# Attention and two MoE layers in one program: unread products in the first tiles, an earlier key copy, and a bound on the narrowing

## The chip, the core and the metric

The kernel runs on one core of a Trainium2 chip. The core has a matmul engine (TensorE, PE in the rows), a vector engine (VectorE, DVE), a scalar engine (ScalarE, ACT), a general engine (GpSimd, POOL) and a queue engine that starts transfers (SyncE, SP). Each runs its own instructions in order; semaphores tie them together. The metric is the device time of one execution in microseconds (us), as the median of several.

## What is computed

Four batches, eight heads, 576 positions, head size 64. Attention with rotated queries and keys feeds two dense layers, all in float32:

```python
q_rot, k_rot = rotate(q), rotate(k)
scores = scale * np.matmul(q_rot, k_rot.transpose(0, 1, 3, 2))
scores = scores - np.max(scores, axis=-1, keepdims=True)
attn = np.exp(scores)
attn = attn / (np.sum(attn, axis=-1, keepdims=True) + 1e-09)
x = np.matmul(attn, v)                      # then to (2304, 512)
h = np.maximum(np.maximum(x @ w1, x @ w2), x @ w3)   # 512 -> 768
x = h @ w_out                                        # 768 -> 512
h = x @ w_in                                         # 512 -> 2048
out = (h * (1.0 / (1.0 + np.exp(-h)))) @ w_out2      # 2048 -> 512
```

## The kernel before

**Attention.** Heads are worked on in pairs; a pair is a batch and two heads. `load_qk` brings queries and keys of a pair, `qk_rope` rotates them (on VectorE for pair 0 and half of pair 1, on GpSimd for the rest), and `qk_turn` transposes them on TensorE into a tile `T` and two small tiles with blocks on the diagonal, `K` (`kd`) and `Q` (`qd`), which serve the last 64 positions of both heads. The tail of a pair (positions 512 to 575) is one more transposition into a PSUM tile `tr`, from which ScalarE copies a part of `T` and the two blocks of `Q`, and VectorE the two blocks of `K`. The two engines' copies out of one PSUM tile follow each other in the order of the program text.

A tile is 128 queries of a pair. The first tiles, numbered here from 0, are tiles 0 and 1 of pair 0, then two of pair 1, two of pair 2 and two of pair 3; behind those come the three remaining ones of each pair. Tile 10 is a small one. `attention` runs one step per tile: `tile_scores` (matmuls L387 and L390 into `s`, of which there is one buffer of three PSUM banks), `tile_max` (VectorE's reduction L400 and two exponentials L407 on ScalarE), `tile_norm` of the tile before (reciprocal L417 and two scalings L419) and `tile_turn` of the one before that: nine transpositions L448 in three groups through `tr`, which has two buffers, each group copied to `pt` by ScalarE (L452) or VectorE (L454). After every two tiles of a pair, `av` multiplies by V (L463, L467).

**The weights.** They come as 64-bit floats. W1, W2 and W3 together are twelve pieces, called pieces 0 to 11 here. `narrowing` takes them to 32 bits in a pipeline, one stage further at each step: `narrow_a` (L214 on ScalarE, and then L216 on GpSimd, or L218 on ScalarE for piece 0), `narrow_b` (L225 and L226 on VectorE), `measure` (L140 on ScalarE, a bound on the size). There are four landing buffers, so the transfer of piece n + 4 waits for L226 of piece n. Six pieces give a scale, by `all_max`, and are then split in a high and a low half of 16 bits (L160 on GpSimd, L163 on VectorE); only then real products of the first layer can run. `prep_w1` does one such step for each tile, two from the ninth on.

**What sets the order.** The program text is recorded, and a scheduler then lays out each engine's order with a model of the time. `tc.issue_after(x)` bars an instruction from being placed before `x` in that order. `last` is a dictionary of such marks: `last["max"]` is the newest row maximum, `last["T"]` the newest copy of `T` by ScalarE. PSUM tiles with the tag `m` (two buffers of the ring `ps_m`) serve `all_max` and the first layer.

Of the kernel before, what the change touches and what calls it, by code (L numbers as in the profile page):

```python
# [7 lines left out]
F32 = mybir.dt.float32  # L8
F16 = mybir.dt.float16
I32 = mybir.dt.int32  # L10
U16 = mybir.dt.uint16
AF = mybir.ActivationFunctionType
# [5 lines left out]
P = 128  # L18
# [4 lines left out]
def fused_kernel(  # L23
# [22 lines left out]
    nc = tc.nc  # L46
# [105 lines left out]
    def flat(t):  # L152
        return t.rearrange("p a b -> p (a b)")
# [183 lines left out]
    def qk_turn(b, hp):  # L337


        t = raw_t.pop((b, hp))  # L340
        T = t_p.tile([P, 576 + 512], F32, tag="T", name="T")
        K, Q = kd[(NP * b + hp) % NK], qd[(NP * b + hp) % NK]
        for i in (1, 0):
            tr = ps_t.tile([P, 512], F32, tag="tr", name="tr")
            for c in range(4):
                behind = tc.issue_after(last["s"]) if b == 0 and hp > 1 else nullcontext()
                with behind:
                    nc.tensor.transpose(tr[:, c * P:(c + 1) * P], flat(t[:, 8 * i + 2 * c:8 * i + 2 * c + 2, :]), ident)
            if i == 0:
                last["T"] = nc.scalar.activation(out=T[:, 0:512], in_=tr, func=AF.Copy, scale=0.125).ins  # L350
            else:
                nc.vector.tensor_copy(out=T[:, 512:1024], in_=tr)
        tr = ps_t.tile([P, 512], F32, tag="tr", name="tr")
        nc.tensor.transpose(tr[:, 0:P], flat(t[:, 16:18, :]), ident)
        nc.scalar.activation(out=T[:, 1024:1088], in_=tr[:, 64:128], func=AF.Copy)
        rs = (slice(0, 64), slice(64, 128))
        for r in rs:
            nc.scalar.activation(out=Q[r, r], in_=tr[r, 0:64], func=AF.Copy, scale=0.125)
        for r in rs:
            last["kd"] = nc.vector.tensor_copy(out=K[r, r], in_=tr[r, 64:128]).ins  # L360
        T_t[b, hp] = T, K, Q


# [11 lines left out]
    def tile_scores(key):  # L375
# [2 lines left out]
        s = ps_s.tile([P, 1536], F32, tag="s", name="s")  # L378
        if t == 4:
            nc.tensor.matmul(s[:, 0:512], Q, T[:, 512:1024], start=True, stop=True)  # L380
            nc.tensor.matmul(s[:, 512:576], Q, T[:, 1024:1088], start=True, stop=True)
            s_t[key] = s
            return
        n = P
# [3 lines left out]
        for g, o in ((0, 0), (1, 1024)):  # L388
            r = slice(64 * g, 64 * g + 64)
            last["s"] = nc.tensor.matmul(s[:, o:o + 512], qs[r], kt[r], start=True, stop=True).ins  # L390
        s_t[key] = s

    def heads(key):
# [27 lines left out]
    def tile_turn(key):  # L421
# [9 lines left out]
        if t == 4:  # L431
# [5 lines left out]
            nc.vector.tensor_copy(out=pt[:, 5:9, o:o + 64], in_=t4[:, :, 1])  # L437
            tr = ps_t.tile([P, 512], F32, tag="tr", name="tr")
            nc.tensor.transpose(tr[:, 0:P], e[:, 448:576], ident)
            nc.tensor.transpose(tr[0:64, P:2 * P], e[:, 512:576], ident)  # L440
            nc.scalar.activation(out=pt[0:64, 4, o:o + 64], in_=tr[0:64, P:P + 64], func=AF.Copy)
            nc.vector.tensor_copy(out=pt[64:128, 4, o:o + 64], in_=tr[64:128, 64:128])
            return
        for j in range(3):
            tr = ps_t.tile([P, 512], F32, tag="tr", name="tr")
            for i in range(3):
                c = 3 * j + i
                nc.tensor.transpose(tr[:, i * n:(i + 1) * n], e[0:n, c * P:(c + 1) * P], ident[0:n, 0:n])  # L448
            to, of = pt[:, 3 * j:3 * j + 3, o:o + n], tr[:, 0:3 * n].rearrange("p (a n) -> p a n", a=3)
            evacs[0] += 1  # L450
            if evacs[0] % 3 == 1 if evacs[0] < 28 else evacs[0] % 3:
# [47 lines left out]
    for b in range(1, B):  # L499
# [3 lines left out]
            at(u - 2, v_max, b, hp)  # L503
        at(u, v_scale, b)

    def attention():

        for j in range(len(tiles) + 4):
# [6 lines left out]
                tile_turn(tiles[j - 2])  # L515
            for f, a in events.pop(j, ()):
                f(*a)
            yield


# [101 lines left out]
    def narrowing(W, stage, srcs, queue, lo=0, hi=None):  # L622
# [3 lines left out]
        for n in range(lo, hi + 3):  # L626
            if n < hi:
                r[n] = queue(n, W, stage(n), srcs[n])
            if lo < n <= hi:
                W.narrow_a(n - 1, r[n - 1], pool=n > lo + 1 or lo > 0)  # L630
            if lo + 2 <= n <= hi + 1:
                with tc.issue_after(last["max"]):
                    W.narrow_b(n - 2, r[n - 2])
# [503 lines left out]
    for hp in range(NP):  # L1137
        load_v(0, hp)
    last["max"] = qk_rope(*pairs[0]).ins
    qk_turn(*pairs[0])  # L1140
    wprep = prep_w1(stage1)
    for j in sorted(e for e in events if e < 0):
        for f, a in events.pop(j):
# [133 lines left out]
```

## Time and profile before

| | us |
|---|---|
| median of 3 runs | 1037.62 |
| lowest, highest | 1037.03, 1039.41 |
| the profiled execution | 1035.59 |
| its span in the profile | 1033.9 |

| engine | busy us | share of the span |
|---|---|---|
| TensorE | 962.4 | 93% |
| VectorE | 688.3 | 67% |
| ScalarE | 616.3 | 60% |
| GpSimd | 489.6 | 47% |

The span is what the profile covers from the first instruction to the last; 1.7 us of the execution lie around it. Times in the rows count from the span's start. Shares are averages over the whole span, while the change touches its first tenth, so the section of rows below has stretches and timelines of that tenth. In a timeline, what stands in brackets is how long the engine was idle before the row and what ended that. TensorE's clock has two levels; the column PEclk gives the granted one as a share of the upper. In the first 20 us the column reads 1.00, since no change of the clock is recorded before; the durations there are those of the lower level (2.08 us for four matmuls L390 that take 1.13 at the upper).

### The profile page before, as it was taken

To read this page: it belongs to the slowest core of one execution; us is meant where nothing else is said; L and a number is where in the kernel's file an instruction comes from. 1 tells how busy PE (TensorE), PEld (TensorE's weight loads), DVE (VectorE), ACT (ScalarE), POOL (GpSimd) and SP (SyncE) were. 2 spreads that over 40 slices of the span, in tenths; PEclk is the share of its full clock that TensorE was granted. 3 is DMA by queue.
4 is the path that set the end of the run, shared out by engine and by line. 5 is a ranking of instruction groups with operands and counts; after the bars stand their busy time and mean duration, and the time that the engine had idled before them with its cause. 6 is when DMAs were issued, how large, how long until landed. Compare 5 with 4: busy or idle time off the path is not lost.

```text
span 1033.9 us, 19511 instructions
## 1 busy us (share of the span) xinstructions
PE 962.4 (93%) x7234; PEld 717.0 (69%) x7234; DVE 688.3 (67%) x1295; ACT 616.3 (60%) x1377; POOL 489.6 (47%) x548
## 2 busy tenths in 40 slices
PE   4677998999999999998999999999999999999997
PEld 2343664666666766655756668777888888888887
DVE  6769877765567655687566646645678767867454
ACT  3778676566666575867767754534455644644352
POOL 6735593961127720354223205536258457346164
PEclk9688999999999999999999999999999999999999
DMA  6943132422334510653444415254345244342201
GB/s 152 280 115 101 33 97 75 129 71 62 102 109 110 137 47 27 189 147 118 144 123 139 143 58 168 82 187 145 128 144 168 92 152 125 108 129 93 90 3 41
DMA packets 126062, 117.99 MB, mean 114 GB/s; under 512 B 47376, under 2 KB 109584, under 8 KB 125968
## 3 DMA queue, kind: packets, MB, share of 16 engines
q1 hardware_dynamic: 124464, 116.03, 37.4%
q8 instruction: 57, 0.93, 0.4%
q10 hardware_dynamic: 1504, 0.72, 0.3%
q14 instruction: 37, 0.30, 0.1%
HBM read 90.51 MB, written 26.21 MB: 113 GB/s over the span
## 4 chain that ended last, share of the span: by engine, by line
PE 62%; DVE 9%; ACT 6%; POOL 6%; DMA 6%; issue 3%; SPq 1%; ACTq 0%; DVEq 0%; POOLq 0%
PE m L538 18%; PE xp L467 6%; PE m L946 5%; PE s L390 5%; PE tr L448 5%; PE mb L946 4%; POOL gsum L893 4%; PE mg L538 3%; PE c L1010 3%; PE a L1010 2%; PE b L1010 2%; POOL yr L981 2%; DVE nb L400 1%; PE d L1010 1%; DVE g L898 1%
## 5 line engine op out<-in xcount | busy, mean ns | idle before, releaser
L538 PEld LDWEIGHTS <-w 128*128 128x128 f16 x1632 | 157.3, 98 | 68.8 <-issue 27.8
L538 PE MATMUL m<-x,w 128*128 128x256 f16 (+1 forms) x1336 | 189.7, 288 | 9.9 <-ACT t L554 4.0
L1010 PEld LDWEIGHTS <-g 128*128 128x128 f16 x1485 | 145.7, 98 | 19.9 <-issue 2.3
L946 PEld LDWEIGHTS <-w8s 128*128 128x128 f16 x1344 | 131.4, 98 | 20.3 <-issue 4.8
L400 DVE TENSOR_REDUCE nb<-s 128x2 f32<-128x1152 f32 (+1 forms) x80 | 98.7, 1234 | 49.4 <-PE s L390 39.5
L212 POOL TENSOR_SCALAR z<-z 128x256 uint16<-128x256 uint16 x64 | 56.0, 875 | 159.2 <-DVE z L211 148.4
L407 ACT ACTIVATE e<-s,nb 128x576 f32<-128x576 f32 x144 | 105.1, 735 | 29.0 <-DVE nb L400 24.9
L419 ACT ACTIVATE e<-e,rec 128x576 f32<-128x576 f32 x144 | 104.5, 768 | 17.8 <-DVE rec L417 17.5
L448 PE MATMUL tr<-ident,e 128*128 128x128 f32 x576 | 97.4, 289 | 14.2 <-ACT T L350 6.2
L787 POOL TENSOR_TENSOR z<-z 128x128 f32<-128x128 f32 (+1 forms) x96 | 59.0, 634 | 105.5 <-DMA z<-zwo 38.4
L448 PEld LDWEIGHTS tr<-ident,e 128*128 128x128 f32 x576 | 69.8, 147 | 50.0 <-issue 13.4
L946 PE MATMUL m<-yr,w8s 128*128 128x256 f16 x768 | 90.8, 273 | 3.7 <-DVE t L952 3.7
L452 ACT ACTIVATE pt<-tr 128x384 f32<-128x384 f32 x119 | 56.8, 486 | 47.9 <-PE tr L448 47.7
L467 PE MATMUL xp<-pt,vd 128*64 128x256 f32 (+1 forms) x512 | 84.6, 419 | 0.0
L390 PE MATMUL s<-T 64*128 64x512 f32 x256 | 83.7, 698 | 0.0
L960 POOL TENSOR_TENSOR z<-t 128x256 f32<-128x256 f32 x32 | 28.0, 875 | 95.8 <-DVE t L952 55.9
L946 PE MATMUL mb<-yr,w8s 128*128 128x256 f16 x576 | 69.9, 274 | 2.3 <-ACT yr L158 2.1
L538 PE MATMUL m<-h,wo 128*128 128x256 f16 (+1 forms) x448 | 64.9, 286 | 0.1
L898 DVE SCALAR_TENSOR_TENSOR g<-gsum,sg,g 128x1024 f16<-128x1024 f32 x36 | 49.1, 1373 | 22.1 <-ACT g L897 21.6
L538 PEld LDWEIGHTS <-wo 128*128 128x128 f16 x512 | 49.3, 98 | 16.9 <-issue 4.0
L897 ACT ACTIVATE g<-gsum,sg 128x1024 f16<-128x1024 f32 x36 | 40.7, 1140 | 32.8 <-POOL gsum L893 32.8
L330 POOL TENSOR_TENSOR w<-qk,sin_sb 128x384 f32<-128x384 f32 (+1 forms) x44 | 45.7, 1058 | 30.4 <-DMA qk<-in_q_dram 16.0
(231 smaller groups left out, 1910.8 us busy)
## 6 DMA issues: line engine op xcount, KB each, us to landing
w8s<-w8scr SPq DMA_DIRECT2D x64, 448.0 KB, 4.2
z<-in_moe_w_in_dram SPq DMA_DIRECT2D x32, 256.0 KB, 3.2
z<-in_moe_w_out_dram SPq DMA_DIRECT2D x32, 256.0 KB, 3.3
w<-in_moe_w_dram SPq DMA_DIRECT2D x6, 768.0 KB, 6.0
wo<-in_moe_w_dram SPq DMA_DIRECT2D x6, 768.0 KB, 4.6
qk<-in_q_dram SPq DMA_DIRECT2D x32, 128.0 KB, 3.0
vd<-in_v_dram SPq DMA_DIRECT2D x16, 256.0 KB, 3.0
zwi<-z SPq DMA_DIRECT2D x32, 128.0 KB, 3.1
```

Source lines behind the costliest of these rows:

```text
L390: last["s"] = nc.tensor.matmul(s[:, o:o + 512], qs[r], kt[r], start=True, stop=True).ins
L400: x = nc.vector.tensor_reduce(out=nb[:, 0:m], in_=both(s, 0, 960, 576) if m > 1 else s[:, 0:576], op=ALU.max, axis=AX.X, negate=True)
L407: x = nc.scalar.activation(out=e[:, HK[g]], in_=s[:, SK[g]], func=AF.Exp, bias=nb[:, g:g + 1], accum_out=sm[:, g:g + 1])
L419: nc.scalar.activation(out=e[:, HK[g]], in_=e[:, HK[g]], func=AF.Copy, scale=r[:, g:g + 1])
L448: nc.tensor.transpose(tr[:, i * n:(i + 1) * n], e[0:n, c * P:(c + 1) * P], ident[0:n, 0:n])
L452: nc.scalar.activation(out=to, in_=of, func=AF.Copy)
L467: nc.tensor.matmul(xp[r, 0:n], v4[:, g, c, :], pt[:, c + 5 * g, :], start=False, stop=(c == 3))
L538: nc.tensor.matmul(ps[:, 0:n], l, r, start=(first and i == 0), stop=(not more and i == len(passes) - 1))
L787: nc.gpsimd.tensor_tensor(out=z[:, o], in0=z[:, x], in1=z[:, y], op=op)
L898: nc.vector.scalar_tensor_tensor(out=l, in0=x, scalar=sg_t[jb], in1=h, op0=ALU.mult, op1=ALU.subtract)
L946: nc.tensor.matmul(o, l, r, start=(i == 0), stop=(i == len(passes) - 1))
L1010: x = nc.tensor.matmul(ps, l, r, start=first, stop=last_, skip_group_check=True)
```

## The change

Four things are done, and three marks are added to `last` for them: `pe_q`, the transposition of a pair's tail; `pe_s`, the last matmul of the newest scores; `pe_t`, the last transposition of the newest tile turned.

- `warm(n)` issues n matmuls of 128x128 by 128x256 in float16. Both operands are the identity matrix read as float16. They write a PSUM tile that nothing reads.
- 50 of them stand ahead of the first pair's transpositions, 10 behind those, 7 behind the scores of each of the tiles 0 to 10, and 7 behind the transpositions that the same steps issue from the third on: 200 in all.
- For the first pair alone, the copies of `K` come before the three copies by ScalarE out of the same tile, instead of after them.
- `narrow_a` gets `issue_after(last["T"])`.

```diff
-        nc.tensor.transpose(tr[:, 0:P], flat(t[:, 16:18, :]), ident)
-        nc.scalar.activation(out=T[:, 1024:1088], in_=tr[:, 64:128], func=AF.Copy)
+        last["pe_q"] = nc.tensor.transpose(tr[:, 0:P], flat(t[:, 16:18, :]), ident).ins
         rs = (slice(0, 64), slice(64, 128))
-        for r in rs:
-            nc.scalar.activation(out=Q[r, r], in_=tr[r, 0:64], func=AF.Copy, scale=0.125)
+
+        def tails():
+            nc.scalar.activation(out=T[:, 1024:1088], in_=tr[:, 64:128], func=AF.Copy)
+            for r in rs:
+                nc.scalar.activation(out=Q[r, r], in_=tr[r, 0:64], func=AF.Copy, scale=0.125)
+
+        first_pair = b == 0 and hp == 0
+        if not first_pair:
+            tails()
         for r in rs:
             last["kd"] = nc.vector.tensor_copy(out=K[r, r], in_=tr[r, 64:128]).ins
+        if first_pair:
+            tails()
...
+    idle = ident.bitcast(F16)
+
+    def warm(n, after=None):
+
+        ps = ps_m.tile([P, 512], F32, tag="m", name="m")
+        with tc.issue_after(after) if after else nullcontext():
+            for _ in range(n):
+                nc.tensor.matmul(ps[:, 0:256], idle[:, 0:P], idle, start=True, stop=True)
+
     def attention():
...
+            if j < 11:
+                warm(7, last["pe_s"])
+                if j > 1:
+                    warm(7, last["pe_t"])
             yield
...
             if lo < n <= hi:
-                W.narrow_a(n - 1, r[n - 1], pool=n > lo + 1 or lo > 0)
+                with tc.issue_after(last["T"]):
+                    W.narrow_a(n - 1, r[n - 1], pool=n > lo + 1 or lo > 0)
...
     last["max"] = qk_rope(*pairs[0]).ins
+    warm(50)
     qk_turn(*pairs[0])
+    warm(10, last["pe_q"])
     wprep = prep_w1(stage1)
```

Since the scheduler lays out the order anew, instructions move on all engines. In the rows below a name ends in the number of its tensor in that build; lines of the kernel after lie further down than those of before (L407 is L416 there, L416 is L425, L419 is L428, L400 is L409, L417 is L426, L454 is L463, L360 is L366, L471 is L480).

ScalarE from the exponentials of tile 1 to those of tile 2, before:

```order
L407 ACTIVATE e_322,sm_323<-s_316,nb_320 128x576 x2
L214 ACTIVATE w_0_138<-w_0_295 128x768
L416 ACTIVATE rec_347<-sm_323 128x2
L218 ACTIVATE w_0_295<-w_0_295 128x768
L419 ACTIVATE e_322<-e_322,rec_347 128x576 x2
L214 ACTIVATE w_0_138<-w_1_312 128x768
L140 ACTIVATE junk_394,w1m_136<-w_0_138 128x768
L214 ACTIVATE w_0_138<-wo_0_141 128x768
L350 ACTIVATE T_368<-tr_375 128x512
L407 ACTIVATE e_343,sm_344<-s_337,nb_341 128x576 x2
```

and after, up to the first narrowing:

```order
L416 ACTIVATE e_392,sm_393<-s_386,nb_390 128x576 x2
L425 ACTIVATE rec_425<-sm_393 128x2
L428 ACTIVATE e_392<-e_392,rec_425 128x576 x2
L350 ACTIVATE T_446<-tr_453 128x512
L416 ACTIVATE e_421,sm_422<-s_415,nb_419 128x576 x2
L214 ACTIVATE w_0_138<-w_0_357 128x768
```

The copy of `T` for pair 2 and the exponentials of tile 2 stood behind five narrowing steps, and now stand ahead of the first.

VectorE around the maximum of tile 2 (`nb_341`), before:

```order
L454 COPY pt_352<-tr_358 128x3x128
L225 TENSOR_SCALAR w_0_138<-w_0_138 128x768
L417 RECIPROCAL rec_347<-rec_347 128x2
L226 SCALAR_TENSOR_TENSOR w_0_138<-w_0_295,w_0_138 128x768
L400 TENSOR_REDUCE nb_341<-s_337 128x2
L150 TENSOR_REDUCE vmax_309<-vd_0_129 128x1
```

and around that of tiles 2 and 3 (`nb_419`, `nb_494`), after:

```order
L463 COPY pt_430<-tr_441 128x3x128
L426 RECIPROCAL rec_425<-rec_425 128x2
L409 TENSOR_REDUCE nb_419<-s_415 128x2
L150 TENSOR_REDUCE vmax_371<-vd_0_129 128x1
L352 COPY T_446<-tr_447 128x512
L306 TENSOR_REDUCE vm_0_520<-vmax_371 128x1
L119 TENSOR_REDUCE amax_524<-m_522 1x1
L225 TENSOR_SCALAR w_0_138<-w_0_138 128x768
L366 COPY kd_0_124<-tr_459 64x64 x2
L426 RECIPROCAL rec_500<-rec_500 128x2
L409 TENSOR_REDUCE nb_494<-s_490 128x2
L226 SCALAR_TENSOR_TENSOR w_0_138<-w_0_357,w_0_138 128x768
```

Piece 0's L226 stood ahead of the maximum of tile 2, and now stands behind that of tile 3.

VectorE up to the maximum of tile 4 (`nb_452`), before:

```order
L226 SCALAR_TENSOR_TENSOR w_0_138<-wo_0_141,w_0_138 128x768
L130 TENSOR_SCALAR ve_433<-m_428 128x1
L454 COPY pt_463<-tr_469 128x3x128
L454 COPY pt_352<-tr_416 128x3x128
L131 TENSOR_SCALAR ve_433<-ve_433 128x1
L417 RECIPROCAL rec_458<-rec_458 128x2
L132 TENSOR_SCALAR vs_434<-ve_433 128x1
L133 TENSOR_SCALAR vi_435<-ve_433 128x1
L400 TENSOR_REDUCE nb_452<-s_448 128x2
```

and after (`nb_562`):

```order
L226 SCALAR_TENSOR_TENSOR w_0_138<-w_1_382,w_0_138 128x768
L132 TENSOR_SCALAR vs_528<-ve_527 128x1
L133 TENSOR_SCALAR vi_529<-ve_527 128x1
L463 COPY pt_573<-tr_579 128x3x128
L226 SCALAR_TENSOR_TENSOR w_0_138<-wo_0_141,w_0_138 128x768
L426 RECIPROCAL rec_568<-rec_568 128x2
L480 SCALAR_TENSOR_TENSOR x_589<-xp_590,vs_528,x_589 128x256
L409 TENSOR_REDUCE nb_562<-s_558 128x2
```

In both, three pieces' L226 are through before the maximum of tile 4, but after, those of pieces 1 and 2 lie in the last eight rows ahead of it, where before only piece 2's did.

## Rows read from the trace of the kernel before

**Rows 1.** Stretches: length; busy us (instructions) PE, PEld, DVE, ACT, POOL; PEclk; DMA.

```profile
36.00:45.00 9.00, 5.99 (x19) 3.35 (x20) 7.18 (x12) 7.61 (x20) 7.32 (x5) 0.50 1.01 289
80.00:103.00 23.00, 15.74 (x79) 8.07 (x76) 22.68 (x30) 19.03 (x41) 12.52 (x8) 0.86 0.36 114
100.00:150.00 50.00, 46.63 (x324) 32.30 (x324) 36.96 (x69) 34.88 (x86) 36.12 (x33) 0.97 0.19 55
```

**Rows 2.** Timeline of TensorE: start, us, line, operation, out<-in, count [idle before].

```profile
9.95 1.09 PE L348 MATMUL tr<-ident,qk 128*128 128x128 f32 x4 [9.95 <-DVE qk L334]
...
14.26 0.77 PE L387 MATMUL s<-kd,T 128*128 128x128 f32 x2 [1.50 <-DVE kd L360]
14.96 2.08 PE L390 MATMUL s<-T 64*128 64x512 f32 x4
...
35.83 0.90 PE L448 MATMUL tr<-ident,e 128*128 128x128 f32 x3 [6.17 <-ACT T L350]
...
49.85 1.95 PE L467 MATMUL xp<-pt,vd 128*64 128x256 f32 x16
...
52.10 0.49 PE L387 MATMUL s<-kd,T 128*128 128x128 f32 x2
52.51 1.13 PE L390 MATMUL s<-T 64*128 64x512 f32 x4
...
103.20 0.59 PE L387 MATMUL s<-kd,T 128*128 128x128 f32 x2 [0.29 <-ACT e L407]
...
109.44 1.47 PE L538 MATMUL m<-x,w 128*128 128x256 f16 x12
```

**Rows 3.** Timeline of ScalarE, same columns.

```profile
29.83 1.93 ACT L218 ACTIVATE w<-w 128x768 uint16<-128x768 uint16 x1
...
50.52 0.71 ACT L407 ACTIVATE e<-s,nb 128x576 f32<-128x576 f32 x1
...
58.21 0.74 ACT L407 ACTIVATE e<-s,nb 128x576 f32<-128x576 f32 x1 [1.00 <-DVE nb L400]
...
61.49 0.60 ACT L350 ACTIVATE T<-tr 128x512 f32<-128x512 f32 x1 [1.49 <-PE tr L348]
...
67.52 0.74 ACT L407 ACTIVATE e<-s,nb 128x576 f32<-128x576 f32 x1 [2.38 <-DVE nb L400]
...
74.33 0.92 ACT L214 ACTIVATE w<-w 128x768 f32<-128x768 f32 x1 [0.99 <-DMA w<-in_moe_w_dram]
...
75.52 0.73 ACT L407 ACTIVATE e<-s,nb 128x576 f32<-128x576 f32 x1
```

**Rows 4.** Timeline of VectorE, same columns.

```profile
13.66 0.46 DVE L360 COPY kd<-tr 64x64 f32<-64x64 f32 x2 [1.68 <-ACT qd L358]
14.15 1.43 DVE L330 TENSOR_TENSOR w<-qk,sin_sb 128x512 f32<-128x512 f32 x2
...
17.74 1.36 DVE L400 TENSOR_REDUCE nb<-s 128x2 f32<-128x1152 f32 x1
...
33.39 1.34 DVE L400 TENSOR_REDUCE nb<-s 128x2 f32<-128x1152 f32 x1
...
44.62 2.42 DVE L226 SCALAR_TENSOR_TENSOR w<-wo,w 128x768 int32<-128x768 int32 x1
...
48.39 1.35 DVE L400 TENSOR_REDUCE nb<-s 128x2 f32<-128x1152 f32 x1
...
60.66 0.94 DVE L226 SCALAR_TENSOR_TENSOR w<-w,w 128x768 int32<-128x768 int32 x1
```

**Rows 5.** Timeline of GpSimd, same columns.

```profile
36.31 2.10 POOL L216 TENSOR_SCALAR w<-w 128x768 uint16<-128x768 uint16 x1
38.49 4.66 POOL L216 TENSOR_SCALAR wo<-wo 128x768 uint16<-128x768 uint16 x2
44.59 1.90 POOL L216 TENSOR_SCALAR w<-w 128x768 uint16<-128x768 uint16 x1 [1.44 <-ACT rec L416]
...
70.03 1.91 POOL L216 TENSOR_SCALAR w<-w 128x768 uint16<-128x768 uint16 x1 [10.62 <-ACT w L214]
```

More of the change, by code (lines that the diff above doesn't have):

```diff
@@ L380, in tile_scores @@
             nc.tensor.matmul(s[:, 0:512], Q, T[:, 512:1024], start=True, stop=True)
-            nc.tensor.matmul(s[:, 512:576], Q, T[:, 1024:1088], start=True, stop=True)
+            last["pe_s"] = nc.tensor.matmul(s[:, 512:576], Q, T[:, 1024:1088], start=True, stop=True).ins
             s_t[key] = s
@@ L390, in tile_scores @@
             last["s"] = nc.tensor.matmul(s[:, o:o + 512], qs[r], kt[r], start=True, stop=True).ins
+        last["pe_s"] = last["s"]
         s_t[key] = s
@@ L439, in tile_turn @@
             nc.tensor.transpose(tr[:, 0:P], e[:, 448:576], ident)
-            nc.tensor.transpose(tr[0:64, P:2 * P], e[:, 512:576], ident)
+            last["pe_t"] = nc.tensor.transpose(tr[0:64, P:2 * P], e[:, 512:576], ident).ins
             nc.scalar.activation(out=pt[0:64, 4, o:o + 64], in_=tr[0:64, P:P + 64], func=AF.Copy)
@@ L447, in tile_turn @@
                 c = 3 * j + i
-                nc.tensor.transpose(tr[:, i * n:(i + 1) * n], e[0:n, c * P:(c + 1) * P], ident[0:n, 0:n])
+                last["pe_t"] = nc.tensor.transpose(tr[:, i * n:(i + 1) * n], e[0:n, c * P:(c + 1) * P], ident[0:n, 0:n]).ins
             to, of = pt[:, 3 * j:3 * j + 3, o:o + n], tr[:, 0:3 * n].rearrange("p (a n) -> p a n", a=3)
```

## The prediction, made before the result was known

> **What bounds the kernel now.** The first view is the table of stretches. From 100 us on TensorE is busy 46.63 of 50 us; from 80 to 103 us VectorE is busy 22.68 of 23, and TensorE only 15.74; from 36 to 45 us the granted clock is 0.50, the lower of TensorE's two levels (1.2 against 2.4 GHz) [rows 1]. So the program has two parts. Up to about 103 us it is a loop over attention tiles in which TensorE often waits; behind that TensorE is the bound, and what starts earlier there ends earlier. The change is worth what it moves the start of tile 12, at 103.20 us [rows 2].
>
> Then the timelines, engine by engine. One tile is a ring: scores on TensorE, the row maximum on VectorE, two exponentials on ScalarE, and only then the next scores, since the score tile has a single buffer. Tile 0 starts at 14.26, tile 12 at 103.20 [rows 2], so a round takes (103.20 - 14.26) / 12 = 7.4 us. The ring itself is shorter. Scores at the upper level are two pieces of 0.49 and 1.13 that overlap a little, about 1.55; at the lower level they are 0.77 and 2.08, about 2.75 [rows 2]. The maximum is 1.35 [rows 4]; two exponentials of 0.73, each with its read of the sum, end some 1.6 after the first starts [rows 3]; for the handovers I take 0.25. That is 4.75. The other 2.65 of a round are lower clock and queueing behind the narrowing of W1.
>
> **The key copies.** They wait 1.68 us for ScalarE's copies of the query blocks [rows 4], though they read only the transposed tail. Copied first, they end about 1.4 earlier. VectorE then goes on to the rotation of pair 1, from 14.15 to the first maximum at 17.74 [rows 4]: 3.6 us that do not shrink. So the first maximum starts at 17.74 - 1.4 = 16.3. The first scores are ready before that: ten products stand in front of them, 10 x 1.47/12 = 1.2 us by the row of twelve products [rows 2], but the key copies hide part of it, and at the upper level the scores themselves take 1.2 less. The 50 products at the very start stand in the 9.95 us in which TensorE has nothing [rows 2]: at the upper level they take 50 x 0.12 = 6 us, at the lower one 12. I take them as hidden; the worst is some 2 us of delay to the first transposes, of which the wait of the second ones for VectorE's rotation hides most.
>
> **The bound on the narrowing.** Before, VectorE's maximum of tile 2 stands behind the L226 of weight piece 0, and this waits for ScalarE's 1.93 us L218: it starts at 33.39 [rows 3, 4]. On ScalarE the narrowing stands ahead of the copy T of pair 2, and TensorE waits 6.17 us for that copy [rows 2]. After, as the first two pairs of orders above show, the maxima of tiles 2 and 3 and the copy T go first. Two rounds of 4.75 from 16.3 put the maximum of tile 2 at 25.8, **7.6 earlier**.
>
> That does not last. GpSimd rotates pairs 1 to 3 until 36.31 and nothing moves that; its narrowing of pieces 1, 2 and 3 ends at 38.4, 40.8 and 43.1 [rows 5]. In VectorE's new order the L226 of pieces 1 and 2 stand ahead of the maximum of tile 4 (the third pair of orders). Piece 2 is ready at 40.8. Its L226 takes 2.42 when GpSimd narrows beside it, from 44.59, and 0.94 when GpSimd is idle [rows 4, 5]; I take 2.42, since piece 3 follows on GpSimd at once. With the reciprocal and one low part behind it (0.6 together, an estimate) the maximum of tile 4 starts at 43.9 against 48.39: the lead is **4.5 us** there, not 7.6.
>
> **From tile 4 to tile 7.** The exponentials of tile 4 start at 45.75, when the maximum is done (45.25) and ScalarE has ended the bound of a piece; before it was 50.52. From there to those of tile 7 at 75.52 are 25.0 us, in which ScalarE waits 1.00 + 1.49 + 2.38 + 0.99 = 5.9 in four places [rows 3], and some 0.3 in small ones: 18.8 of work. In the new order the same stretch holds two more L214 (0.92 each [rows 3]) and two small evacuations fewer, for which I take half of that each: 19.7. Of the waits, 1.5 come back where a copy waits for the transposes of tile 4, as these now stand behind seven unread products (7 x 0.12 = 0.86), and 0.9 for the ring itself; 2.4 together. So the exponentials of tile 7 start at 45.75 + 19.7 + 2.4 = 67.85, a lead of **7.7 us**. The wait of 0.99 for a weight transfer moves along with piece 5, whose L226 sets that transfer free.
>
> **From tile 8 on.** VectorE is full from 80 to 103 us [rows 1] and keeps the same instructions, so nothing is won or lost there; 24 real products run ahead of tile 12 before and after. Fourteen unread products in each of these tiles are 1.7 us of TensorE's idle time, 7 us in this stretch: hidden. Behind tile 12 the order differs in details up to about the 1,260th of 6,710 matmuls (some 270 us, an estimate from that share), and not at all after. TensorE's 3.4 idle us from 100 to 150 [rows 1] may come out otherwise, 2 us either way. Nothing in this part hangs on absolute time, so the lead is kept.
>
> **The sum.** I give 0.1 to further handovers: 1035.59 - 7.6 = 1028.0 for this execution (its span of 1033.9 and 1.7 around it). The median of the runs, 1037.62, lies 2.03 above it, which gives **1030.0 us**.
>
> **Unknown prices.** How well the products hold the clock, no row shows. From below they are worth nothing, and scores stay near 2.75 in half the tiles; as the ring does not bind from tile 4 on, that takes 1 to 3 us from the lead. From above, all tiles run at the upper level, as the ring above supposes. I take the upper end, since the nearest row is that of tile 5, whose scores take 1.13 right after dense work [rows 2], and keep both for the range. Should ScalarE have no wait left at all, the lead is 10 to 12 us: the low end.
>
> **Rivals.** First, *the front is bound elsewhere*: GpSimd's rotation, and then a ScalarE that is nearly full, allow no more than tile 4's lead, and the two further L214 and the products eat that down to 1 or 2 us: 1036. For it: the lead does fall to 4.5 at tile 4. Against it: the 5.9 us of ScalarE's own waits. 10%.
>
> Second, *VectorE and GpSimd block each other*. L226 takes 1.5 us more beside GpSimd's narrowing [rows 4, 5]. The new order packs the narrowing of pieces 3 to 7 into less time, so more of these ten VectorE steps meet one of GpSimd's; at 1.5 each, half of them on the path, that is 7.5 us, the whole lead: 1037. 6%. The Trainium skill, page "SBUF — State Buffer", section "Who interferes with whom", says that a VectorE instruction with two SBUF inputs and a GpSimd one that reads SBUF share a port pair, and that whichever comes second waits until the first ends. By that rule, with which the 2.42 agrees, closer packing costs time.
>
> Third, the slower side: *the unread products stand in the way at the lower clock*. A tile then needs on TensorE 2.75 of scores, nine transposes (0.90 for three [rows 2], about 2.1 in all), half of a product with V (1.95 at the upper level [rows 2], so 1.95 for half at the lower) and fourteen products of 0.24, 3.4: 10.2 us. It decides once this passes the round of 7.4; five such tiles cost 14, less the lead of 7.6: 1044. Against it: the clock was low where TensorE was sparse (busy 5.99 of 9 us at 0.50 [rows 1]) and the products fill just that. 6%.
>
> Fourth, *the new order loses behind tile 12*: the second half of W1 and the first groups of the first layer interleave otherwise, and TensorE's idle time there, 3.4 us in the first 50, grows by the whole lead or a little more: 1038 to 1041. 5%, half of it slower.
>
> **Chances.** The forecast, 1026 to 1034, has 73%. Faster by over 0.2% (about what a measurement of this kernel can tell from no change, here 2.1 us) gets this and a part of the first two rivals: 79%. Within it: 12%. Slower: 9%. The range 1024.5 to 1036.5 leaves out some 4% below and 14% above.
>
> **What would show it.** In the profile after: key copies that do not wait for the query copies; the first maximum near 16.3; that of tile 2 near 26; that of tile 4 near 44, behind an L226 that waits for GpSimd; tile 7's exponentials near 68; tile 12 near 95.5; a granted clock near 1.00 up to there. I am wrong if tile 4's maximum is later than 46, if the clock stays at 0.50, or if tile 12 is early and the lead is gone by 270 us.

## The result and the profile after

The change made the kernel slower: 1043.24 us median (1041.38 to 1047.03, six runs) against 1037.95 for the kernel before in the same runs (1036.51 to 1039.82, six runs). The ratio is 1.0053, with a 95% interval of 1.003 to 1.0076. The forecast was 1030.0, and the range ended at 1036.5. The profiled execution of the kernel after took 1042.60 us, with a span of 1040.9. Its page begins so (span; busy time, share and instructions of each engine):

```profile
span 1040.9 us, 19926 instructions
PE 983.5 (94%) x7434; PEld 734.0 (71%) x7434; DVE 688.2 (66%) x1295; ACT 617.4 (59%) x1377; POOL 489.2 (47%) x548
```

The table of stretches of the kernel after, with the columns of [rows 1], and one stretch that [rows 1] doesn't have, from 150 to 200 us:

```profile
36.00:45.00 9.00, 6.34 (x44) 3.84 (x44) 9.00 (x15) 7.97 (x17) 6.04 (x3) 1.00 0.89 215
80.00:103.00 23.00, 17.71 (x96) 10.12 (x93) 20.24 (x30) 17.48 (x40) 9.10 (x6) 0.86 0.29 94
100.00:150.00 50.00, 46.66 (x327) 32.20 (x325) 40.54 (x74) 34.24 (x85) 30.10 (x28) 0.97 0.20 57
150.00:200.00 50.00, 41.75 (x224) 24.71 (x225) 27.66 (x62) 23.29 (x63) 35.77 (x37) 0.83 0.31 82
```

That last stretch in the kernel before:

```profile
150.00:200.00 50.00, 45.25 (x293) 28.83 (x292) 38.82 (x84) 34.37 (x95) 31.75 (x34) 0.97 0.40 107
```

The front is what the change was to make it: from 36 to 45 us the clock is 1.00 where it was 0.50 [rows 1]. What is new is the stretch from 150 to 200 us. TensorE is busy 3.5 us less, at a clock of 0.83 instead of 0.97, and starts 69 matmuls fewer; VectorE does 11 us less. A part of the program in which the prediction saw nothing that hangs on time has become the worst one.

The simplest view of where the time went is the start of each tile's scores, before against after. I call the difference the lead.

| tile | before | after | lead |
|---|---|---|---|
| 4 | 45.67 | 42.75 | 2.9 |
| 7 | 70.79 | 61.73 | 9.1 |
| 11 | 92.64 | 89.00 | 3.6 |
| 12 | 103.20 | 98.85 | 4.4 |
| 19 | 152.69 | 143.35 | 9.3 |
| 20 (first of batch 1) | 163.34 | 152.93 | 10.4 |
| 21 | 167.94 | 164.93 | 3.0 |
| 23 | 181.92 | 189.51 | -7.6 |
| 24 | 188.17 | 201.24 | -13.1 |
| 34 | 272.01 | 279.97 | -8.0 |

Not all of these starts are like for like. At tile 19 the lead looks 2.8 us larger than it is, since the new order has done 24 products of the first layer less by then (24 take 2.78 us there; at tiles 15 and 16 it is 12): of 9.3 us 6.5 are a lead. The scores of tile 20 are in two halves after the change, and the 18 products with V, which before stand ahead of all of them, lie between the halves. The last scores of tile 20 before:

```profile
163.75 1.13 PE L390 MATMUL s<-T 64*128 64x512 f32 x4
```

and after:

```profile
159.95 1.12 PE L398 MATMUL s<-T 64*128 64x512 f32 x2
```

They end at 161.07 in place of 164.88, a lead of 3.8 and not of 10.4. From tile 31 on almost the same work stands ahead of a tile in both. So the front gained up to 9 us, of which 6.5 were left at tile 19; 3.5 of these went by tile 21, and 11 more between tile 21 and tile 34. A lead is read from one execution of each kernel; how much of it differs from one execution to the next was not measured.

### The profile page after: what moved, and what is told of

It reads as the page before. It is cut to its first block, busy times and chain, and to the rows that moved or that the text cites. A ratio compares the mean times of both kernels' runs of the same rounds, so it can differ in the third digit from the quotient of the medians.

```text
span 1040.9 us, 19926 instructions
## 1 busy us (share of the span) xinstructions
PE 983.5 (94%) x7434; PEld 734.0 (71%) x7434; DVE 688.2 (66%) x1295; ACT 617.4 (59%) x1377; POOL 489.2 (47%) x548
## 4 chain that ended last, share of the span: by engine, by line
PE 64%; POOL 9%; DVE 8%; ACT 5%; DMA 5%; issue 4%; SPq 1%; DVEq 0%; POOLq 0%; ACTq 0%
PE m L560 19%; PE xp L476 6%; PE s L398 5%; PE m L969 5%; PE tr L457 5%; PE mb L969 4%; POOL gsum L916 4%; PE mg L560 3%; PE c L1033 3%; PE b L1033 2%; PE a L1033 2%; POOL yr L1004 1%; PE s L395 1%; PE d L1033 1%; PE xp L472 1%
## 5 line engine op out<-in xcount | busy, mean ns | idle before, releaser
L416 ACT ACTIVATE e<-s,nb 128x576 f32<-128x576 f32 x144 | 105.2, 736 | 45.4 <-DVE nb L409 36.1
L409 DVE TENSOR_REDUCE nb<-s 128x2 f32<-128x1152 f32 (+1 forms) x80 | 98.7, 1234 | 48.3 <-PE s L398 40.2
L428 ACT ACTIVATE e<-e,rec 128x576 f32<-128x576 f32 x144 | 104.5, 769 | 15.4 <-DVE rec L426 14.4
L457 PE MATMUL tr<-ident,e 128*128 128x128 f32 x576 | 94.5, 282 | 8.4 <-DVE pt L463 3.0
L476 PEld LDWEIGHTS xp<-pt,vd 128*64 128x64 f32 x512 | 37.2, 139 | 35.4 <-issue 17.4
```

Source lines behind the costliest of these rows:

```text
L409: x = nc.vector.tensor_reduce(out=nb[:, 0:m], in_=both(s, 0, 960, 576) if m > 1 else s[:, 0:576], op=ALU.max, axis=AX.X, negate=True)
L416: x = nc.scalar.activation(out=e[:, HK[g]], in_=s[:, SK[g]], func=AF.Exp, bias=nb[:, g:g + 1], accum_out=sm[:, g:g + 1])
L428: nc.scalar.activation(out=e[:, HK[g]], in_=e[:, HK[g]], func=AF.Copy, scale=r[:, g:g + 1])
L457: last["pe_t"] = nc.tensor.transpose(tr[:, i * n:(i + 1) * n], e[0:n, c * P:(c + 1) * P], ident[0:n, 0:n]).ins
L476: nc.tensor.matmul(xp[r, 0:n], v4[:, g, c, :], pt[:, c + 5 * g, :], start=False, stop=(c == 3))
```

## Where the time went

**The start of the loss: GpSimd.** Between the front and batch 1, GpSimd splits the second half of W1 into high parts (L160, six of them, by the scale `sw11s`) and then rotates three pairs of batch 1 (L330, L331, L334). The rows of GpSimd before (start, us, line, operation, out<-in, count, idle before):

```profile
109.37 0.90 POOL L160 TENSOR_SCALAR w<-w,sw11s 128x768 f16<-128x768 f32 x1 [5.50 <-DVE rec L417]
...
120.17 0.90 POOL L160 TENSOR_SCALAR w<-w,sw11s 128x768 f16<-128x768 f32 x1 [1.33 <-PE tr L448]
121.04 3.81 POOL L330 TENSOR_TENSOR w<-qk,sin_sb 128x384 f32<-128x384 f32 x3
```

and after:

```profile
109.17 0.91 POOL L160 TENSOR_SCALAR w<-w,sw11s 128x768 f16<-128x768 f32 x1 [10.39 <-DVE sw11i L133]
...
125.95 0.91 POOL L160 TENSOR_SCALAR w<-w,sw11s 128x768 f16<-128x768 f32 x1 [2.01 <-DVE rec L426]
126.82 3.81 POOL L330 TENSOR_TENSOR w<-qk,sin_sb 128x384 f32<-128x384 f32 x3
...
155.53 1.34 POOL L216 TENSOR_SCALAR w<-w 128x512 uint16<-128x512 uint16 x1
...
158.53 1.35 POOL L216 TENSOR_SCALAR w<-w 128x512 uint16<-128x512 uint16 x1
```

Two things are to be seen. The first split does not start earlier, though tile 12 does: GpSimd waits 10.39 us for the scale. The maxima of W1 were ready at 100.65 (106.52 before), but in the new order the small product that transposes them stands on TensorE behind the scores of tile 12 and 18 products with V, at 105.42. And the six splits then take 17.7 us in place of 11.7, because each waits for VectorE's low part of the piece before, and VectorE's new order has more between these; ahead of the fifth stands an L216 of 1.79 us as well. So GpSimd starts the rotation of batch 1 **5.8 us later** (126.82 against 121.04), while TensorE is about 5 us early (tiles 15 and 16 lead by 7.6 and 5.5, less 1.4 for the 12 products). The lead never reached GpSimd.

**The second half of the loss: the bound holds WO1 too.** `narrowing` is one function for W1 and WO1. With `issue_after(last["T"])` WO1's last pieces come behind the copies of `T` of batch 1, and GpSimd's two last L216 (155.53 and 158.53 above) fall in between the steps of its third rotation; before they stood at 142.41 and 153.60. VectorE of the kernel after waits for both, with the maximum of tile 20 queued behind:

```profile
156.90 0.69 DVE L226 SCALAR_TENSOR_TENSOR wo<-w,wo 128x512 int32<-128x512 int32 x1 [4.26 <-POOL w L216]
159.92 0.69 DVE L226 SCALAR_TENSOR_TENSOR wo<-w,wo 128x512 int32<-128x512 int32 x1 [2.33 <-POOL w L216]
...
161.87 1.36 DVE L409 TENSOR_REDUCE nb<-s 128x2 f32<-128x1152 f32 x1
```

That maximum loses 0.8 us by it, as its scores end at 161.07. The larger delay is that of WO1's scale: it comes at 170.40 (167.62 before), since VectorE takes the maximum of tile 20 ahead of the last steps for it, and TensorE the scores of tile 21. TensorE's order has changed further on too: in front of tile 23 stand 36 matmuls of the second layer instead of 28, in front of tile 24, 324 products of both layers instead of 270. They meet WO1's splits before these are done:

```profile
178.26 0.50 PE L560 MATMUL m<-h,wo 128*128 128x256 f16 x3 [0.50 <-POOL wo L160]
179.80 0.61 PE L560 MATMUL m<-h,wo 128*128 128x256 f16 x4 [1.04 <-DVE wo L163]
181.22 0.61 PE L560 MATMUL m<-h,wo 128*128 128x256 f16 x4 [0.81 <-POOL wo L160]
182.73 1.89 PE L560 MATMUL m<-h,wo 128*128 128x256 f16 x8 [0.90 <-DVE wo L163]
```

Four waits of 3.25 us together; the last eight products take 1.89, which is the lower clock, and tile 23's scores stand behind it all at 189.51. From tile 21 to tile 23 the clock is 0.79 to 0.80, where it was 1.00 before.

## The experiments

Theory A is that the bound on WO1 costs the lead, theory B that the unread products do, by the order and the clock that they leave behind; theory G, formed after the first four kernels, that GpSimd's late rotation does, theory H that something else binds the start of batch 1. Since the scheduler lays out the whole order anew for each kernel, an edit is never alone: what it moved is told where the argument needs it.

Each kernel below ran beside the kernel before on the same chip, so two kernels are best compared by their ratios to it. The letters: P the unread products, K the key copies first, B the bound on W1 and WO1, B1 the bound on W1 alone, S a step of my own, the six splits of W1's second half on ScalarE instead of GpSimd. The lead is that of the profiled execution at tiles 6, 12, 21 and 33; a rotation's end is the end of GpSimd's last step of the three pairs of batch 1.

| kernel | median us | ratio to before (95%) | lead at 6, 12, 21, 33 | rotation ends |
|---|---|---|---|---|
| before | 1038.0 to 1038.6 | | | 157.0 |
| P K B (the change) | 1043.24 | 1.0053 (1.003 to 1.0076) | 9.4, 4.4, 3.0, -8.5 | 161.5 |
| P K B1 | 1036.98 | 0.9981 (0.9962 to 1.0) | 8.4, 2.8, 2.2, 1.0 | 160.6 |
| P K | 1036.42 | 0.9977 (0.996 to 0.9995) | 7.1, 2.7, 1.2, -0.1 | 160.1 |
| 60 of P, K B | 1038.84 | 0.9994 (0.9979 to 1.0009) | 5.2, 4.1, 2.9, 3.0 | 160.1 |
| B | 1039.54 | 1.0007 (0.9986 to 1.0028) | 2.0, -7.4, -3.8, -3.6 | 164.1 |
| P | 1046.55 | 1.0079 (1.0051 to 1.0107) | 2.9, -3.8, -6.4, -7.7 | 167.5 |
| K | 1040.83 | 1.0024 (1.0004 to 1.0044) | 2.3, -4.0, -5.9, -4.7 | 167.3 |
| P K B1 S | 1030.91 | 0.9931 (0.9909 to 0.9954) | 8.2, 2.3, 7.6, 6.3 | 129.8 |
| S | 1038.09 | 1.001 (0.9991 to 1.0028) | 1.6, 0.8, -0.8, -0.8 | 133.1 |
| P K B S | 1029.65 | 0.9917 (0.9892 to 0.9942) | 7.6, 2.0, 7.3, 6.0 | 130.4 |
| P K S | 1030.02 | 0.9918 (0.9889 to 0.9947) | 7.9, 4.0, 8.8, 7.5 | 130.9 |
| K B1 S | 1041.49 | 1.0027 (1.001 to 1.0044) | 1.5, -7.3, -5.1, -6.4 | 138.0 |
| 60 of P, K B1 S | 1032.99 | 0.9955 (0.9937 to 0.9972) | 4.4, 0.0, 4.4, 3.0 | 133.0 |

### Is it the bound on WO1?

P K B1, the change with the bound taken from WO1:

```diff
-                with tc.issue_after(last["T"]):
+                with tc.issue_after(last["T"]) if W is W1 else nullcontext():
                     W.narrow_a(n - 1, r[n - 1], pool=n > lo + 1 or lo > 0)
```

> The changed kernel, with the bound on the narrowing kept for W1 and taken from WO1. Theory A (the bound was meant for the start, but also holds WO1's narrowing back, since both weights go through one function; with the first copies of batch 1 in front of them, the last two GpSimd pieces of WO1 fall in between the rotations of batch 1, and VectorE and then TensorE wait for them): the lead of 10.4 us at tile 20 is kept, tile 24 starts near 180 instead of 201, 1027 to 1032 us. Theory B (it is not the bound but the unread products: they leave the later work in another order and at another clock whatever WO1 does): the lead still falls to below zero between tiles 20 and 24, 1040 us or more. Half way (1034 to 1038) would say that both take part.

Measured 1036.98, 6 us less than the change (7.5 by the ratios). The loss from tile 21 to tile 24 is gone (2.2 there, 0.4 at tile 24, where the change falls to -13.1), although 34 matmuls of the second layer stand in front of tile 23 here. But the lead of 9.0 at tile 19, 6.2 like for like, still shrinks to 2.3 at tile 20. So the bound on WO1 is worth the 6 us, and theory A explains half of what is missing: the other half is lost before, with or without it.

The 60 products at the start only, sevens left out (P in the table holds all 200):

```diff
-            if j < 11:
-                warm(7, last["pe_s"])
-                if j > 1:
-                    warm(7, last["pe_t"])
```

> The changed kernel with only the 50 + 10 unread products at the start; the sevens of the first eleven tiles are left out, the bound still holds for W1 and WO1. TensorE's order of real products around tiles 22 to 28 is that of before here (54 down products and no further up products at tile 24, not 72 and 252 up), but GpSimd's last two pieces of WO1 still stand between batch 1's rotations. Theory A in its strict form (late WO1 itself costs): the lead is lost between tiles 20 and 24 all the same, 1036 to 1044 us. Theory A' (late WO1 costs only because TensorE then takes other products ahead of the scores): most of the lead at tile 20 is kept, 1029 to 1034 us. Theory B: 1034 or less, with a front some 2 to 4 us later than with the sevens, if these held the clock.

Measured 1038.84, the same as before, and a number of strict theory A; the tiles say otherwise. Here WO1's last pieces are about as late on GpSimd as in the change (L216 at 154.14 and 157.14), TensorE's order from tile 22 on is that of before, and a lead of 2.9 at tile 21 is 2.9 at tile 24. WO1's scale comes at 164.72, where the change has it at 170.40. So late pieces alone don't cost what is lost between these tiles; what is left for it is the other order, which came with them in the change, with the later scale (A'). The step at the change of batches, from 8.0 like for like at tile 19 to 2.9 at tile 21, is there all the same.

P K, no bound at all:

> The changed kernel without the bound: unread products and the key copies first only. Theory A: no loss behind tile 20 (the lead there is what the total gains); the front is as before up to tile 4, since VectorE's maximum of tile 2 stands behind the narrowing again, so a lead of 2 to 6 us at tile 12 from the clock alone: 1032 to 1036 us. Theory B: the lead, whatever it is, is lost at tiles 20 to 24 by some 15 us: 1045 us or more.

Measured 1036.42, near theory A's range and far from theory B's. But the front has almost all of its lead without the bound (7.1 against 8.4 at tile 6), and again nothing is left at tile 24 (-0.6).

B alone, the bound added to the kernel before:

> The kernel before with the bound alone, for both weights as in the change. Theory A: the front gains some 4 to 7 us, and the late WO1 takes them and more: 1036 to 1044 us, with VectorE waiting for GpSimd's last pieces of WO1 near 155 us. Theory B: without unread products nothing is lost at tiles 20 to 24, 1029 to 1034 us.

Measured 1039.54, the same as before. Theory A was wrong about the place: the bound alone gains 2.0 at tile 6, is at -7.4 by tile 12, and gets 3.7 of these back by tile 21.

### What makes the front's lead?

P alone (key copies where they were), and K alone:

> The kernel before with the 200 unread products alone (no bound, key copies where they were). Theory F1 (the lead that the change has at tile 6, 9.4 us, comes from the products, which hold TensorE's clock up, since the bound alone left 2.0 there): a lead of 5 to 8 us at tile 6. Theory F2 (it comes from the order of the key copies, which lets VectorE and ScalarE go on earlier): under 2 us at tile 6. In both cases at most 3 us are left at tile 21, and the time is 1035 to 1039 us.

Measured 1046.55, the slowest of all and far above what either theory gave: 2.9 at tile 6, between the two, and -3.8 at tile 12.

> The kernel before with the key copies of the first pair first, and nothing else. Theory F1: a lead of 0 to 2 us at tile 6. Theory F2: 5 us or more at tile 6. The total 1036 to 1039 us either way, unless the other order of WO1's pieces, which comes with it, matters.

Measured 1040.83: 2.3 at tile 6. Neither F1 nor F2 holds as written. The products and the key copies make more together (7.1) than one by one: in the order that the scheduler builds for P alone VectorE's maximum of tile 3 stands at 39.00, behind an L226, as that of tile 2 did in the kernel before; with K as well it goes ahead, at 35.00. P and K both lose most at the change of batches, 5.8 and 4.3 us like for like from tile 19 to tile 21, though they come there with no lead; their rotations end latest.

### Is it GpSimd?

The splits of W1's second half on ScalarE, first on top of P K B1 (`split` gets the engine as an argument; not shown here):

```diff
-                    lows = [W1.split(i, w1_scale[g][0], later=True)]
+                    lows = [W1.split(i, w1_scale[g][0], later=True, engine="act" if i >= half else "pool")]
```

> The change with the bound for W1 alone, and the six splits of W1's second half (the high parts, L160) on ScalarE in place of GpSimd. Theory G (the lead of the front is lost at the start of batch 1 because GpSimd's rotation of it stands behind those splits, which end at 126.7 us in place of 121.0): the rotation starts near 110 us, ends before 150, tile 21 starts before 160, with a lead of 6 us or more, and the whole takes 1031 to 1034 us. Theory H (batch 1's start is bound elsewhere, by VectorE or by the arrival of WO1): the rotation ends early too, but tile 21 starts near 165 again and the time is 1035 to 1039 us.

Measured 1030.91: theory G by its number, with a lead of 7.6 at tile 21 (160.37) and 6.3 at tile 33. It is not the lead of the front carried through, as the prediction and the theory had it: that is 2.3 at tile 12 and 2.5 like for like at tile 19, less than the 6.2 of P K B1. From tile 19 to tile 21 P K B1 S gains 5.1, and P K B1 loses 4.0. The rotation starts even earlier than expected, at 95.13:

```profile
95.13 4.06 POOL L330 TENSOR_TENSOR w<-qk,sin_sb 128x384 f32<-128x384 f32 x3
...
125.54 4.27 POOL L334 TENSOR_TENSOR qk<-qk,w 128x384 f32<-128x384 f32 x3
```

What GpSimd's late rotation costs is shown by VectorE from the maximum of tile 19 to the maximum of WO1's bounds (L240), nearly the same steps in both kernels. In P K B1, where GpSimd rotates until 160.6:

```profile
146.17 0.74 DVE L409 TENSOR_REDUCE nb<-s 128x1 f32<-128x576 f32 x1
146.84 0.95 DVE L225 TENSOR_SCALAR wo<-wo 128x512 int32<-128x512 int32 x1
147.71 1.55 DVE L226 SCALAR_TENSOR_TENSOR wo<-w,wo 128x512 int32<-128x512 int32 x1
149.18 1.21 DVE L585 TENSOR_TENSOR h<-t,h 128x256 f16<-128x256 f32 x1
...
153.68 0.92 DVE L146 TENSOR_SCALAR wo1m<-wo1m 128x6 int32<-128x6 int32 x1
154.51 0.41 DVE L585 TENSOR_TENSOR h<-t,h 128x256 f16<-128x256 f32 x1
154.84 0.95 DVE L147 TENSOR_SCALAR wo1m<-wo1m 128x6 int32<-128x6 int32 x1
155.83 0.23 DVE L451 COPY pt<-tr 64x64 f32<-64x64 f32 x1
156.09 0.66 DVE L696 TENSOR_SCALAR wo1m<-wo1m,ratio 128x3 f32<-128x3 f32 x1
156.78 0.16 DVE L240 TENSOR_REDUCE wm<-wo1m 128x1 f32<-128x6 f32 x1
```

with these steps of GpSimd beside the last of them, about 1 us each:

```profile
151.33 3.24 POOL L330 TENSOR_TENSOR w<-qk,sin_sb 128x384 f32<-128x384 f32 x3
154.53 3.15 POOL L331 TENSOR_TENSOR qk<-qk,cos_sb 128x384 f32<-128x384 f32 x3
```

In P K B1 S, where GpSimd has nothing to do from 146.84 to 161.10:

```profile
149.13 0.75 DVE L409 TENSOR_REDUCE nb<-s 128x1 f32<-128x576 f32 x1
149.79 0.42 DVE L225 TENSOR_SCALAR wo<-wo 128x512 int32<-128x512 int32 x1
150.12 0.69 DVE L226 SCALAR_TENSOR_TENSOR wo<-w,wo 128x512 int32<-128x512 int32 x1
150.73 0.42 DVE L585 TENSOR_TENSOR h<-t,h 128x256 f16<-128x256 f32 x1
...
153.74 0.17 DVE L146 TENSOR_SCALAR wo1m<-wo1m 128x6 int32<-128x6 int32 x1
...
154.27 0.16 DVE L147 TENSOR_SCALAR wo1m<-wo1m 128x6 int32<-128x6 int32 x1
154.47 0.23 DVE L696 TENSOR_SCALAR wo1m<-wo1m,ratio 128x3 f32<-128x3 f32 x1
154.73 0.16 DVE L240 TENSOR_REDUCE wm<-wo1m 128x1 f32<-128x6 f32 x1
```

The first takes 10.8 us from the start of the first row to the end of the last, the second 5.8. (Key copies and a copy of `pt`, 0.9 us, stand inside the first and ahead of the second; a wait of 0.7 for ScalarE is in the second alone.) A step that works from SBUF to SBUF and starts while GpSimd is in one of its steps is longer: L225 0.95 against 0.42, L226 1.55 against 0.69, L585 1.21 against 0.42, and the steps on six numbers a row 0.92 and 0.95 against 0.17. The second L585, at 154.51, starts 0.02 ahead of GpSimd's L331 and takes 0.41. The maximum, which reads PSUM, takes the same. The copy `pt` (L451) comes at 155.83 in the first and at 152.11 in the second, though the maximum of tile 19 was 3 us later there. TensorE in P K B1 waits for VectorE:

```profile
152.32 0.30 PE L448 MATMUL tr<-ident,e 128*128 128x128 f32 x1 [2.91 <-DVE kd L366]
...
156.11 0.90 PE L457 MATMUL tr<-ident,e 128*128 128x128 f32 x3 [2.20 <-DVE pt L451]
```

From 146 to 156 us TensorE is busy 4.14 us there, and 8.73 in P K B1 S. A part of the loss is the clock that goes with this: 0.66 from 151 to 161 us, where P K B1 S has 1.00 from 150 to 160. The rows of the batch's last transpositions and of its products with V (from the first row above on) add up to 6.75 us in place of 4.65. In the kernel before VectorE's steps lie behind the end of the rotation (157.0) for the most part and take 5.5 us, from 156.40 to 161.86:

```profile
156.40 0.75 DVE L400 TENSOR_REDUCE nb<-s 128x1 f32<-128x576 f32 x1
...
161.70 0.16 DVE L240 TENSOR_REDUCE wm<-wo1m 128x1 f32<-128x6 f32 x1
```

So this is the loss at the change of batches: VectorE did there, beside the rotation, what it used to do behind it. All kernels of the table agree, and they show that a lead is not needed for it. Like for like, the seven without S whose rotation ends 9.0 to 18.1 us behind the start of tile 19 lose 1.3 to 5.8 us from tile 19 to tile 21 against the kernel before, where it ends 4.3 behind; P and K are among them, which come with no lead. The six with S, whose rotation ends 15 us or more ahead of tile 19, gain 4.9 to 5.1 there (S alone 2.7), and K B1 S, which comes 10.1 us late, gains as much as P K S, which comes 3.8 early. The Trainium skill, page "SBUF — State Buffer", section "Who interferes with whom", says that a VectorE step with two SBUF inputs and a GpSimd step that reads SBUF exclude each other; L226 and the first L585 agree with it.

S alone, on the kernel before:

> The kernel before with nothing but the six splits of W1's second half on ScalarE. Theory G: the rotation of batch 1 ends 10 us or so earlier than 157 us, tile 21 starts 2 to 5 us earlier than 167.9, since TensorE has more to do between (24 more products of the first layer are used up earlier): 1034 to 1037 us. Theory H: no change, 1037 to 1039 us. If ScalarE becomes the late one there (six steps of about 0.9 us in a stretch where it is busy 35 of 50 us), it is slower, 1040 us.

Measured 1038.09, no change: theory H's number, but not its reason. At the change of batches S alone gains 2.7 us, and it comes there 3.5 late. Between tiles 12 and 15, with the same products done, its lead goes from 0.8 to -3.7: the rotation, now from 98.40 to 133.09, runs beside VectorE's low parts of W1 (the six L163 of the second half take 8.5 us together, 6.8 before), and the clock is 0.67 from 100 to 110 us and 0.74 from 110 to 120, where it was 0.83 and 1.00. In the three pairs of kernels that differ by S alone (P K B1, P K B, P K), S costs 2.8 to 4.1 us up to tile 19 as well. It pays where the rotation would else end late, and gains no more than it costs where it didn't. What of this cost is VectorE, the clock or ScalarE's six splits was not separated.

The change as it is, with S:

> The change as it is, with the bound on both weights, and the six splits of W1's second half on ScalarE. If the bound on WO1 costs because GpSimd's pieces of WO1 fall in between the rotations of batch 1 (theory A), it costs nothing here, where the rotation is done by 140 us: 1030 to 1033 us, as with the bound on W1 alone (1030.9). If holding WO1's narrowing back is what costs, whatever GpSimd does, the 6 us stay: 1035 to 1038 us.

Measured 1029.65, with the bound on WO1 still there. One edit that has nothing to do with the front takes the changed kernel from 1043.24 to 0.4 us from the forecast. That it lands there is chance: of its lead of 7.3 at tile 21, 4.9 are gained at the change of batches, where the forecast had nothing. The 6 us of the bound on WO1 vanish with it: no rotation is left for the pieces to fall into, and TensorE's order there is that of P K B1 again (34 matmuls of the second layer in front of tile 23, 282 products in front of tile 24). The two were not separated.

P K S, no bound:

> Unread products, key copies first, the six splits on ScalarE, no bound at all. With GpSimd out of the way the front's lead should count, and the bound gave the front 1 to 2 us (8.4 against 7.1 at tile 6): 1031 to 1033 us. If the bound is the source of most of the lead, as the prediction had it, 1034 to 1037 us.

Measured 1030.02, no different from the two with a bound. So beside S the bound is worth nothing that can be measured, as it was between P K and P K B1.

K B1 S, without a product, and with the 60 at the start:

> Key copies first, bound for W1, the six splits on ScalarE, and no unread product. Theory F1 (the products hold TensorE's clock in the front): the clock is near 0.8 up to 100 us again, the lead at tile 6 is 3 us or less, 1034 to 1038 us. If the products are not needed (order alone makes the lead): 1030 to 1033 us.

Measured 1041.49, slower than expected: the clock is 0.50 from 36 to 45 us again and 0.79 from 45 to 80, where all products give 0.62 and 1.00, and the lead at tile 12 is -7.3.

> As the kernel with the splits on ScalarE and the bound for W1, with only the 60 unread products at the start, without the sevens. Theory F1: a lead of about 5 us at tile 6 (as in the run with the 60 alone), 1031 to 1035 us, between none and all of them.

Measured 1032.99, between, as expected. So once GpSimd is out of the way the products are worth 10.6 us (1041.49 against 1030.91; 10.0 by the ratios), of which the 60 at the start bring 8.5 (7.5 by the ratios); alone, on the kernel before, they cost 8. F1 holds by its number, not quite by its reason: with the 60 the clock is 0.78 from 20 to 36 us, lower than the 0.88 without them, and 0.85 against 0.79 from 45 to 80. A part of what they bring is the order that the scheduler builds with them; the two were not separated.

## Why the prediction was wrong, step by step

- **What bounds the kernel.** Two parts, a front loop and a stretch bound by TensorE, "what starts earlier there ends earlier". This failed. The second part begins with a change of batches at which TensorE waits for VectorE, and VectorE for GpSimd. GpSimd's 36.12 of 50 us [rows 1] hide that it is busy 9.66 us or more of each 10 from 120 to 150 us, until the rotation ends at 157.0. I read a busy share of 46.63 of 50 on TensorE as a bound and didn't ask what GpSimd's queue did there.
- **The key copies.** Right in themselves: they wait 0.42 us, for TensorE alone, and end 1.3 earlier (forecast 1.4). But "3.6 us that do not shrink" grew to 4.7:

```profile
12.37 0.46 DVE L366 COPY kd<-tr 64x64 f32<-64x64 f32 x2 [0.42 <-PE tr L354]
12.85 2.01 DVE L330 TENSOR_TENSOR w<-qk,sin_sb 128x512 f32<-128x512 f32 x2
...
17.56 1.36 DVE L409 TENSOR_REDUCE nb<-s 128x2 f32<-128x1152 f32 x1
```

  The two L330 take 2.01 against 1.43 [rows 4]. They now lie beside GpSimd's L331 of the same pair (12.86 to 14.72, itself 1.86 instead of 1.41 us), which before was all but over when they began. The first maximum is at 17.56, not at 16.3. It is the same contention as above, in the small.
- **The bound on the narrowing.** The order came as read, the sizes did not: tile 2's maximum at 28.54 instead of 25.8 (33.39 before [rows 4]). The scores of tile 2 themselves start at 26.95, later than before (26.15): at 22.61 seven unread products took 1.68 us, at the lower clock, ahead of the transpositions of tile 0. The runs without the bound show that the wrong part of the change got the credit: P K has a lead of 4.5 at tile 3 and 7.1 at tile 6, B alone 0.1 and 2.0.
- **Tile 4 to tile 7.** About right: tile 4's maximum at 44.74 (forecast 43.9), its exponentials at 46.65 (45.75), those of tile 7 at 66.46 (67.85), a lead of 9.1 where 7.7 was forecast. The stretch between the two took 19.8 us, not 22.1.
- **From tile 8 on.** "Nothing is won or lost there" failed by 4.7 us: 9.1 at tile 7, 4.4 at tile 12. VectorE is not full there any more (20.24 of 23 us). Tile 10's scores end at 82.2, but its maximum waits until 86.14 behind two L226 of 1.42 and 2.41 us and an L163 that the new order puts first; before it came at 90.94, 1.4 behind its scores. The step from tile 10 to tile 11 takes 3.7 us of the lead; another 2.2 go between tiles 7 and 8, which is not accounted for here:

```profile
82.81 2.41 DVE L226 SCALAR_TENSOR_TENSOR w<-w,w 128x768 int32<-128x768 int32 x1
...
86.14 0.74 DVE L409 TENSOR_REDUCE nb<-s 128x1 f32<-128x576 f32 x1
```

- **Behind tile 12.** "The lead is kept" is the step that decided, and it failed twice, as the runs show: at the change of batches, by GpSimd's late rotation (6.5 us at tile 19 become 3.0 at tile 21; P K B1 loses 4.0 there, and with S the same stretch gains 5.1), and by the bound on WO1 with the order that came with it (3.0 at tile 21 become -8.0 at tile 34; 6 us of the time). The order of TensorE is the same from tile 34 on, at 272 us, as the prediction had it (its 270 does not follow from its share of 1,260 in 6,710, which gives 194). The step rested on the real products being the same in number; I counted TensorE's queue and didn't put the other queues of the stretch from 100 to 200 us beside it, though the change moves a call that WO1 shares.
- **The rivals.** The fourth, an order that loses behind tile 12, came nearest, at 5% and priced at "the whole lead or a little more"; the lead went and 8 us on top. It looked for the loss in TensorE's idle time of the first 50 us, which did not grow (46.66 us busy against 46.63); the loss lies in the 50 us behind. The second, VectorE and GpSimd in each other's way, was right about the mechanism, but I looked for it in the front and priced it there. The third, products in the way at the lower clock, did not decide: the front gained with them, and in the kernel with S they are worth 10.6 us.

**What stays open.** Near 470 us, at the change to a later batch, some of the kernels lose 1.5 to 4.4 us more: P K B1 falls from 1.0 at tile 60 to -3.4 at tile 62. Those whose clock from 460 to 500 us is 1.00, as before (B, P, and 60 of P with K B1 S), lose nothing; the others are at 0.91 to 0.96. The stretch from 470 to 475 us, before and in P K B1:

```profile
470.00:475.00 5.00, 4.73 (x34) 3.39 (x35) 4.20 (x13) 4.84 (x14) 2.85 (x6) 1.00 0.16 59
```

```profile
470.00:475.00 5.00, 4.13 (x13) 2.01 (x14) 3.28 (x8) 4.29 (x12) 1.71 (x5) 0.52 0.17 50
```

TensorE had been busy 1.50 of the 5 us ahead of that in P K B1, and 2.47 before. No experiment was made on it. How much of the loss between tiles 21 and 34 of the change is WO1's late scale and how much TensorE's other order was not separated. Nor was it tried why P alone loses its 2.9 us between tile 6 and tile 12, or whether placing the small product for W1's scale ahead of the products with V would do without S.

## What to carry to other kernels

A lead on one engine says little about the next change of phase: before writing "the lead is kept", follow every engine, not only the bound one, through that change, and look for the queue with next to no idle time (here GpSimd, 121 to 157 us). Compare only starts that have the same work ahead of them. Where an edit sits in a function that several callers share, each caller is a part of the change. And if two engines get in each other's way, a shift of one against the other is itself a cost: price the overlap that the shift makes, at the place where it makes it.

The version that beats both kernels is the change with the second half's splits on ScalarE: 1029.65 us, 0.9917 of before (0.9892 to 0.9942); without the bound it is the same within the error.

## What I had not expected of the hardware

Steps of VectorE on six numbers a row took 0.17 us with GpSimd idle and 0.77 to 0.95 beside its rotation (P K B1): four of them in a row (L145, L146, L147, L696) each ended 0.03 us behind the GpSimd step that they ran beside, whatever their own work. In the kernel before those of WO1 lie where GpSimd is idle; its trace shows the same in one place, a product of two single numbers a row (L676, 168.35) of 0.60 us beside an L160, where its twin at 109.30 (L671) takes 0.16.
